# From a planner to an explicit list: the order of the first part of a kernel on one core, with two edits in its start

## The chip, the core and the metric

The kernel runs on one core of one Trainium2 chip: TensorE (PE, with its weight loads as PEld), VectorE (DVE), ScalarE (ACT), GpSimd (POOL), and SyncE (SP), whose queue issues nearly all transfers. The metric is device microseconds of one execution.

## What is computed

Three layers in a row. First a delta rule over 768 positions, for 4 batches and 8 heads of width 48; then a feed-forward layer with a hard-swish gate, then a layer of 8 experts of which each token takes the one with the largest logit.

```python
k_n = k / (np.linalg.norm(k, axis=-1, keepdims=True) + 1e-06)
for t in range(S):
    y[:, :, t] = np.einsum('bhd,bhde->bhe', q[:, :, t], state)
    v_old = np.einsum('bhde,bhd->bhe', state, kt)
    state = state + bt[:, :, :, None] * np.einsum('bhd,bhe->bhde', kt, vt - v_old)
h = x @ w_in;  g = h * np.clip(h + 3.0, 0.0, 6.0) / 6.0;  x2 = g @ w_out
out[mask] = gate_w[mask, None] * (np.maximum(x2[mask] @ w1[e], 0.0) @ w2[e])
```

## The kernel before

The positions are cut into 12 steps `s` of 64; each step has two halves `bp` (two batches each), so 24 items `it = 2 s + bp`. Within a step the rule is a triangular system, solved in groups `g` of four items; across steps a state is carried. The kernel has two parts. The first holds the delta rule, and the feed-forward layer's first 7 of 16 blocks for all tokens. The second (from L1459 on) does the other 9 blocks and the experts. Only the first is touched here.

The first part is written as 31 generators, called streams. Each yields its operations one by one (a block of matmuls is one entry), `"need"` entries that hold it until another stream has reached a point, and `"take"` entries that want one of three PSUM banks (L368). The main ones, in the order of the work:

- `kl_stream` loads the keys, `n_stream` (L546) squares them on ScalarE (tile ksq, one buffer), sums the squares on VectorE (`ss`) and makes the norms; `k_stream` (L571) makes `kn` and the block-diagonal pairs `Kbd`, for the first four items on VectorE, later on GpSimd.
- `kt_stream` and `kg_stream` (L591) transpose `Kbd` by DMA; `g_stream` (L603) multiplies keys by keys (block pG, as 64x64 tiles) and copies the result to `Dt` and `MC`.
- `t_stream` (L634), one pass for a group: VectorE transposes `Dt` to `Bt`, GpSimd multiplies `Bt` by beta, ScalarE clears the PSUM tile `Xp`. `s_stream` (L651) solves the triangular system on VectorE in 31 pairs of `sub` and an update of `Xp`. `z_stream` (L668) transposes the result, splits it (`TT`) and multiplies (pZ).
- `chain(bp)` (L827) carries the state: pR (from the second step on), pW twice, pS, each followed by operations on ScalarE and VectorE. `p_stream` and `o_stream` make pP and the output pO, `x_stream` (L909) transposes it (pX) to `xT`; `xo_stream` stores it on SP.
- `m_stream` (L1029) is the feed-forward part: for each step 7 blocks `ph` of 9 matmuls (three entries), each followed by ScalarE `t`, VectorE `tmin` (it writes the tile t again), ScalarE `gH`, GpSimd `gL`, then `py` of 6 matmuls (two entries).
- `wi_stream`, `wo_stream` narrow the weights on VectorE (tile nws: five operations a block, four of them on VectorE) with the small matmuls pwt and pwc; `ahead_stream` (L1001) does the same for the first three blocks of the second part (tile nw). `scale_stream` sums the squares of the values.

`drive` (L1078) decides the order. Before, it keeps a clock of the engines (class Clock, L39): a cost for each operation, the times at which tiles are written and read, a model of the clock of TensorE. At each step it takes, among the streams that could begin first, the one with the smallest due time; the due times stand in DUE (L1121), one row for a stream, and TOL (L1120) says how near two starts must be to compete. `pin` (L164) fixes the order so chosen on each engine. On the chip nothing of this runs: it only sets the order of instructions on the engines and of transfers on SP.

Of the kernel before, what the change touches and what calls it, by code (L numbers as in the profile page):

```python
# [38 lines left out]
class Clock:  # L39


    def __init__(self, tc):
        self.tc, self.last = tc, {}
        self.free = dict(pe=0.0, act=0.0, dve=600.0, pool=3100.0, dma=0.0)
        self.columns = {}
        self.written, self.read, self.bus, self.issue = {}, {}, 0.0, 0.0
        self.slot, self.count, self.parts = {}, {}, {}
        self.runs, self.phase, self.tick, self.warm = [], 0.0, 0, False
        self.mode = 128, False
        self.place, self.end = {}, dict(act=0.0, dve=0.0)  # L50

    def tile(self, pool, shape, dt, tag, bufs, name):
        t = pool.tile(shape, dt, tag=tag, name=name, bufs=bufs)
        n = self.count[tag] = self.count.get(tag, -1) + 1
        self.slot[t.name] = (tag, n % bufs)
        return t

    def keys(self, ap):

        n = ap.name  # L60
        if n in self.parts:
            return [(n, x) for x in self.parts[n](ap)]
        return [self.slot.get(n, n)]

    def cost(self, op):

        n = 1
        for d in (op.ins[0] if "reduce" in op.fn.__name__ else op.out).shape[1:]:
            n *= d
        if "dma" in op.fn.__name__:  # L70
            return 40
        half = (op.ins[-1] if op.eng == "pe" else op.out).dtype in (FP16, FP32R, BF16)
        if op.eng == "pe":
            if op.ins[-1].dtype == FP32R:
                return n / 2.2
            if op.ins[-1].shape[0] <= 64:
                return max(32 if op.ins[-1].shape[0] == 64 else 25.2, n / 2.4) / op.tiles
            return max(25.5, n / 2.4 + 2.5) if half else 0.85 * max(n, 128)
        fn = op.fn.__name__
        pointers = sum(x.free_size() == 1 for x in op.ins[1:])  # L80
        if op.eng == "act":
            return (52 if op.ins[0].space == PSUM else 109) + 95 * (pointers > 0) + 84 * (len(op.outs) > 1) + 0.836 * n
        if op.eng == "dve":
            if half and fn == "tensor_copy":
                return 64 + 0.26 * n
            if fn == "memset":
                return 60 + (0.38 if half else 0.82) * n
            if fn == "transpose":
                return 70 + 1.06 * n
            if fn == "reciprocal":  # L90
                return 70 + 6 * n
            if fn == "tensor_scalar" and op.ins[0].space != PSUM:
                return 66 + 0.52 * n + 60 * (pointers > 0)
            return 70 + (0.52 if all(x.dtype == FP16 for x in op.ins) else 1.04) * n + 60 * (pointers > 0)
        if op.eng == "pool":
            if fn in ("memset", "tensor_copy"):
                return 80 + 0.81 * n
            wide = op.out.dtype == FP32R or op.out.shape[-1] == 32
            return 60 + (2.5 if wide else 2.15) * n
        raise ValueError(op.eng)  # L100

    def places(self, op):

        r, w = {}, (op.out.space, op.out.start_partition())
        for x in op.ins:
            r.setdefault(x.space, x.start_partition())
        return r, w

    def held(self, op):

        r, w = self.places(op)
        now = self.place.setdefault(op.eng, ({}, {}))
        return any(now[0].get(m, x) != x for m, x in r.items()) or now[1].get(w[0], w[1]) != w[1]

    def shared(self, op):

        if op.eng != "dve" or op.fn.__name__ in ("memset", "transpose", "tensor_reduce", "reciprocal"):
            return False
        wide = [x for x in op.ins if x.free_size() > 1]
        sb = [x for x in wide if x.space != PSUM]  # L120
        if op.fn.__name__ in ("tensor_copy", "tensor_scalar"):
            return bool(sb) and op.out.space != PSUM
        return len(sb) > 1

    def unshared(self, t):

        for a, b in reversed(self.runs):
            if b < t:
                break
            if a <= t:  # L130
                return b
        return t

    def matmul(self, op, t):

        n, tick = op.out.free_size(), int((t + self.phase) * 3 / 10240)
        rows = op.ins[-1].shape[0]
        half = op.ins[-1].dtype in (FP16, FP32R, BF16)
        while self.tick < tick:
            self.warm = self.columns.get(self.tick, 0.0) >= (3060 if self.warm else 3350)  # L140
            self.tick += 1
        self.columns[tick] = self.columns.get(tick, 0.0) + n * (1 if half else 2) * rows / 128
        mode, last = (32 if rows <= 32 else 64 if rows <= 64 else 128, op.ins[-1].dtype == FP32R), self.mode
        self.mode = mode
        turn = 90 * (mode[0] != last[0]) + (0 if mode[1] == last[1] else 85 if mode[1] else 13)
        if self.warm:
            return turn + self.cost(op)
        if rows <= 64:
            return turn + max(53.4 if rows == 64 else 42, n / 1.2) / op.tiles
        return turn + (max(27, n / 1.2) if half else 1.7 * max(n, 128))  # L150

    def ready(self, tiles):
        return max([self.free["pe"]] + [self.written.get(k, 0.0) for x in tiles for k in self.keys(x)])

    def start(self, ops):
        t = 0.0
        for op in ops:
            t = max([t] + [self.read.get(k, 0.0) for x in op.outs for k in self.keys(x)] + [self.written.get(k, 0.0) for x in op.ins for k in self.keys(x)])
        t = max(self.free[ops[0].eng], t + {"pe": 54, "pool": 77}.get(ops[0].eng, 33))
        if ops[0].eng in self.end and "dma" not in ops[0].fn.__name__ and self.held(ops[0]):  # L160
            t = max(t, self.end[ops[0].eng] + 13)
        return self.unshared(t) if self.shared(ops[0]) else t
# [9 lines left out]
    def emit(self, ops):  # L172
        t = t0 = self.start(ops)
        for op in ops:
            t += self.cost(op) if op.eng != "pe" else self.matmul(op, t)
            self.pin(op)
        self.free[ops[0].eng] = t
        if "dma" in ops[0].fn.__name__:
            o = ops[0].out
            n = 2 if o.dtype == FP16 else 4  # L180
            turn = "transpose" in ops[0].fn.__name__
            rate = 200 if turn else 170 if n * o.shape[-1] < 512 else 320
            for d in o.shape:
                n *= d
            self.issue = max(self.issue, t) + 600
            self.bus = max(self.bus, self.issue + 650) + n / rate
            if turn:
                self.free["dma"] = self.bus - 870
            elif ops[0].eng == "dma":
                self.free["dma"] = self.issue  # L190
            t = self.bus + 1900
        else:
            if ops[0].eng == "pool":
                if self.runs and t0 - self.runs[-1][1] < 60:
                    self.runs[-1][1] = t + 55
                else:
                    self.runs.append([t0, t + 55])
            t += {"pe": 165, "dve": 84, "act": 95, "pool": 45}[ops[0].eng]
            if ops[0].eng in self.end:
                r, w = self.places(ops[0])  # L200
                now = self.place.setdefault(ops[0].eng, ({}, {}))
                now[0].update(r)
                now[1][w[0]] = w[1]
                self.end[ops[0].eng] = t
        for op in ops:
            for now, used in ((self.written, op.outs), (self.read, op.ins)):
                for k in [k for x in used for k in self.keys(x)]:
                    now[k] = max(now.get(k, 0.0), t)
# [13 lines left out]
def kernel(ctx: ExitStack, tc: tile.TileContext, q, k, v, beta, w_in, w_out, w_gate, w1, w2, out):  # L222
# [137 lines left out]
    with ExitStack() as ax:  # L360
# [717 lines left out]
        def drive(streams):  # L1078
# [6 lines left out]
            def step(x):  # L1085
                while True:
# [4 lines left out]
                    if x[0] != "next":  # L1091
                        break
# [537 lines left out]
```

## Time and profile before

| | us |
|---|---|
| median of three runs | 999.73 |
| lowest, highest | 997.82, 1004.11 |
| the profiled execution | 1003.64 |
| its span, first to last instruction | 1001.9 |
| from the start to L1459 (end of the first part) | 507.6 |

The profile page gives busy times of the engines over the span, and a table of 40 slices. [...] A releaser called "issue" means that the engine waited for nothing that the profile shows.

### The profile page before, as it was taken

The page shows a single profiled execution, that of the slowest core. Times are in us where ns is not written, and L with a number is a line of the kernel's source. Part 1 is how long each engine was busy: PE and PEld are TensorE (multiplying, and loading weights), DVE is VectorE, ACT ScalarE, POOL GpSimd, SP SyncE. Part 2 cuts the span into 40 slices and gives each one's busy share as a digit, 9 for nine tenths or more (in the row PEclk, how much of TensorE's full clock was granted, in tenths as well). Part 3 has the DMA queues.
Part 4 walks back from the last instruction along what each step waited for, and adds up shares of the span by engine and source line. Part 5 has one row for each costly group of instructions (what it writes and reads, how often), then busy time and mean ns, then how long its engine had stood idle before and what let it go on. Part 6 is the DMA issues. An engine that isn't in the chain of part 4 may idle for free.

```text
span 1001.9 us, 27659 instructions
## 1 busy us (share of the span) xinstructions
PE 885.3 (88%) x11454; PEld 819.2 (82%) x11454; DVE 586.2 (59%) x1611; ACT 569.0 (57%) x1195; POOL 433.2 (43%) x446
## 2 busy tenths in 40 slices
PE   1423898889988899999989999999999999999997
PEld 1412888889888798888878899898899999999996
DVE  7888997888979789653487545554534211222221
ACT  4757889779888876755557333323334542455521
POOL 5255565455546524423343204223104936755761
PEclk9999799999999989999999999999999999999999
DMA  7978797996998956566365432332116734434500
GB/s 127 190 145 158 126 179 135 176 139 124 211 198 110 200 112 123 125 155 208 118 218 172 131 93 97 128 96 97 53 61 240 228 105 153 147 114 141 172 21 20
DMA packets 255080, 138.89 MB, mean 139 GB/s; under 512 B 199587, under 2 KB 239845, under 8 KB 254944
## 3 DMA queue, kind: packets, MB, share of 16 engines
q1 hardware_dynamic: 247120, 118.82, 53.5%
q0 software_dynamic: 7280, 17.41, 5.2%
q8 instruction: 91, 1.49, 0.6%
q10 hardware_dynamic: 544, 0.80, 0.2%
q14 instruction: 45, 0.37, 0.1%
HBM read 71.56 MB, written 35.50 MB: 107 GB/s over the span
## 4 chain that ended last, share of the span: by engine, by line
PE 61%; DVE 14%; ACT 8%; issue 7%; DMA 6%; POOL 4%; SPq 0%; POOLq 0%; ACTq 0%
PE ph L1459 11%; PE ph L1250 9%; PE py L36 5%; PE ph L36 5%; PE py L1475 3%; PE py L1474 3%; PE py L1473 3%; PE pz L1238 3%; PE pz L1240 3%; PE pz L1239 3%; DMA KG<-Kbd 2%; DVE Xp L36 2%; DVE sub L36 2%; PE pO L36 2%; PE pW L36 2%
## 5 line engine op out<-in xcount | busy, mean ns | idle before, releaser
L1254 DVE SCALAR_TENSOR_TENSOR hL<-ph,hH 128x384 fp32r<-128x384 f32 (+6 forms) x64 | 36.1, 564 | 163.6 <-ACT hH L1253 163.6
L36 POOL TENSOR_TENSOR gL<-t,gH 128x256 fp32r<-128x256 f32 x84 | 64.6, 769 | 130.8 <-ACT gH L36 122.6
L1253 ACT ACTIVATE hH<-ph 128x384 fp32r<-128x384 f32 (+6 forms) x64 | 31.6, 494 | 104.8 <-PE ph L1250 104.8
L1462 ACT ACTIVATE t<-ph,half 128x512 f32<-128x512 f32 x54 | 37.1, 687 | 76.4 <-PE ph L1459 75.2
L36 PE MATMUL ph<-xTH,wiH 128*128 128x256 f32 x252 | 76.4, 303 | 4.3 <-DVE t L36 3.4
L1419 POOL DMA_INDIRECT slots<-row,di x24 | 23.9, 997 | 125.1 <-DVE di L1411 119.7
L1463 DVE SCALAR_TENSOR_TENSOR t<-t,ph 128x512 f32<-128x512 f32 x54 | 37.1, 686 | 62.8 <-ACT t L1462 62.5
L1238 PE MATMUL pz<-a2H,hH 128*128 128x384 f32 (+1 forms) x216 | 73.2, 339 | 0.4 <-ACT hH L1253 0.4
L36 PE MATMUL ph<-xTL,wiH 128*128 128x256 f32 x252 | 72.2, 286 | 0.7 <-DVE xTL L36 0.7
L1240 PE MATMUL pz<-a2H,hL 128*128 128x384 f32 (+1 forms) x216 | 72.4, 335 | 0.0
L1239 PE MATMUL pz<-a2L,hH 128*128 128x384 f32 (+1 forms) x216 | 72.4, 335 | 0.0
L36 PE MATMUL ph<-xTH,wiL 128*128 128x256 f32 x252 | 71.6, 284 | 0.0
L1271 POOL DMA_INDIRECT out_dram<-yo,rw x29 | 28.0, 967 | 100.7 <-ACT yo L1270 96.5
L1467 DVE TENSOR_TENSOR gL<-t,gH 128x512 fp32r<-128x512 f32 x54 | 47.5, 882 | 32.6 <-ACT gH L1466 32.5
L36 DVE TENSOR_TENSOR Xp<-Xp,sub 128x31 f32<-128x31 f32 (+15 forms) x186 | 64.0, 344 | 2.8
L36 PE MATMUL py<-woH,gH 128*128 128x392 f32 x168 | 64.9, 386 | 0.7 <-issue 0.7
L36 DVE TENSOR_TENSOR sub<-Bt,Xp 128x31 f32<-128x31 f32 (+15 forms) x186 | 61.6, 331 | 2.2
L298 POOL TENSOR_TENSOR a2L<-r,a2H 128x384 fp32r<-128x384 f32 x64 | 62.5, 1009 | 0.0
L36 ACT ACTIVATE t<-ph,half 128x256 f32<-128x256 f32 x84 | 39.6, 471 | 38.4 <-PE ph L36 31.4
L298 POOL TENSOR_TENSOR a1L<-r,a1H 128x512 fp32r<-128x512 f32 x48 | 60.4, 1305 | 0.1
L36 PE MATMUL py<-woH,gL 128*128 128x392 f32 x168 | 58.7, 350 | 0.7 <-POOL gL L36 0.6
L36 DVE SCALAR_TENSOR_TENSOR t<-t,ph 128x256 f32<-128x256 f32 x84 | 35.0, 417 | 40.3 <-ACT t L36 39.3
(318 smaller groups left out, 3141.9 us busy)
## 6 DMA issues: line engine op xcount, KB each, us to landing
r<-in_moe_w_dram SPq DMA_DIRECT2D x32, 768.0 KB, 4.6
slots<-zrow SPq DMA_DIRECT2D x8, 784.0 KB, 6.2
stage<-in_moe_w_in_dram SPq DMA_DIRECT2D x16, 384.0 KB, 3.9
stage<-in_moe_w_out_dram SPq DMA_DIRECT2D x16, 384.0 KB, 3.2
row<-ypart SPq DMA_DIRECT2D x6, 784.0 KB, 4.5
ysave<-row SPq DMA_DIRECT2D x6, 784.0 KB, 3.9
rw<-slots SPq DMA_DIRECT2D x24, 196.0 KB, 3.1
kr<-in_k_dram SPq DMA_DIRECT2D x24, 192.0 KB, 4.6
```

The source lines that it names most:

```text
L36: return self.fn(*self.a, **self.k)
L298: in_order(pool.tensor_tensor(dst[1], src_ap, dst[0].bitcast(FP32), ALU.subtract))
L1238: pe.matmul(o, hh[:, ts_], a2[0][:, fp], start=fp == 0, stop=False)
L1239: pe.matmul(o, hh[:, ts_], a2[1][:, fp], start=False, stop=False)
L1240: pe.matmul(o, hl[:, ts_], a2[0][:, fp], start=False, stop=fp == KF2 - 1)
L1250: pe.matmul(ph, a1[a][:, c, fs], xt[x][:, c, 0:n], start=k == 0, stop=k == 3 * KD - 1)
L1253: act.activation(hH, ph, ACTF.Relu)
L1254: dve.scalar_tensor_tensor(hL, ph, 0.0, hH.bitcast(FP32), ALU.max, ALU.subtract)
L1459: pe.matmul(ph, wi(a, f)[:, c], xt[x][:, c], start=n == 0, stop=n == 3 * KD - 1)
L1462: act.activation(t_, ph, ACTF.Relu, bias=half, scale=1.0 / 6.0)
L1463: dve.scalar_tensor_tensor(t_, t_, 1.0, ph, ALU.min, ALU.mult)
L1467: dve.tensor_tensor(gL, t_, gH.bitcast(FP32), ALU.subtract)
```

## The change

The class Clock becomes Order, which keeps only `tile`, `pin` and `emit`, and the due times become a list: one character for each entry, 2998 in all, naming the stream whose next entry is issued. `need` entries are stepped over as soon as they hold, a `take` is done when its stream's next character comes. The list was found by a search in which the pieces of TensorE's program count as a resource. Two operations in the start change: the tile that holds the first squares, and the engine of the first multiplication of `Bt`. The products of keys keep their 64x64 tiles.

```diff
-class Clock:
+class Order:
     def __init__(self, tc):
         self.tc, self.last = tc, {}
...
     def emit(self, ops):
-        t = t0 = self.start(ops)
         for op in ops:
-            t += self.cost(op) if op.eng != "pe" else self.matmul(op, t)
             self.pin(op)
...
-            yield "take", lambda: clk.ready(inputs) if freeb else None
+            yield "take", lambda: freeb or None
...
-                    sq_ = tmp([128, H, D], FP32, "ksq", 1)
+                    sq_ = tmp([128, H, D], FP32, "ksq" if g or j % 2 else "vsq")
...
-                yield POOL.tensor_tensor(Bt, Bt, bY[:, g].unsqueeze(1).to_broadcast([128, 32, 32]), ALU.mult)
+                yield (POOL if g else DVE).tensor_tensor(Bt, Bt, bY[:, g].unsqueeze(1).to_broadcast([128, 32, 32]), ALU.mult)
...
+            for n in range(len(streams)):
+                step(n)
+            settle()
+            for n in [ALPHABET.index(c) for c in "".join(ORDER)]:
+                if isinstance(now[n], tuple):
+                    assert now[n][0] == "take" and now[n][1]() is not None, (n, now[n])
+                    step(n)
+                assert isinstance(now[n], list), (n, now[n])
+                clk.emit(now[n])
+                step(n)
+                settle()
+            assert not any(now), now
+
+        ALPHABET = "0123456789abcdefghijklmnopqrstu"
+        ORDER = [
+            "jjaaaajkjkkkpbrbbbbbbkpbbrqqsrpobsrbrbrbqsbsbqsqrjsqbqqqqnsqrqsosposqr1n1n0nr0onsnosrrnnrsnqrsnnqqso",
...
+            "uuttututtttuutututuuuututtttttttuttttttttt8ututtttutut9tutttuttttuttutttutttuttutuuttttuuttttutu988",
+        ]
```

The characters stand for the streams in the order of the call of `drive`: 0 and 1 chain, 2 and 3 wc, 4 and 5 o, 6 ql, 7 qt, 8 xo, 9 yo, a kl, b n, c kg, d kt, e q, f p, g x, h t, i z, j and k zero (GpSimd, VectorE), l s, m g, n k, o beta, p v, q scale, r wi, s wo, t m, u ahead.

## Rows read from the trace of the kernel before

**Rows 1.** The page: busy us by engine; TensorE's program queue (packets, MB, share).
```profile
PE 885.3 (88%) x11454; PEld 819.2 (82%) x11454; DVE 586.2 (59%) x1611; ACT 569.0 (57%) x1195; POOL 433.2 (43%) x446
...
q8 instruction: 91, 1.49, 0.6%
```

**Rows 2.** Busy time by stretch: PE, PEld, DVE, ACT, POOL; clock, DMA share, GB/s.
```profile
88.00:124.00 36.00, 24.82 (x713) 23.35 (x714) 30.52 (x88) 28.61 (x55) 19.85 (x17) 0.83 0.84 143
124.00:482.00 358.00, 330.18 (x7516) 308.83 (x7516) 278.65 (x819) 278.41 (x603) 162.99 (x163) 0.98 0.81 154
482.00:508.00 26.00, 22.52 (x132) 19.03 (x131) 14.75 (x40) 13.24 (x32) 10.17 (x13) 0.93 0.44 140
508.00:1002.00 494.00, 483.96 (x2710) 447.48 (x2708) 189.37 (x440) 196.37 (x389) 198.46 (x206) 0.99 0.39 125
...
197.00:200.50 3.50, 3.50 (x55) 3.24 (x49) 3.27 (x9) 2.64 (x9) 0.00 (x0) 0.51 0.78 247
...
487.00:491.00 4.00, 4.00 (x19) 4.00 (x19) 0.59 (x2) 1.10 (x3) 1.01 (x3) 0.57 0.98 302
```

**Rows 3.** The same view, from the start to two points on VectorE.
```profile
0.00:36.13 36.13, 8.83 (x100) 7.45 (x102) 26.90 (x88) 17.44 (x42) 17.00 (x23) 1.00 0.83 144
...
0.00:87.09 87.09, 23.86 (x389) 20.46 (x389) 72.02 (x226) 51.52 (x119) 41.70 (x48) 1.00 0.83 150
```

**Rows 4.** Groups of VectorE instructions, 0 to 51.2 us: busy us, mean ns, idle before.
```profile
L36 DVE CAST W<-idq 32x256 f16<-32x256 f32 x8 | 3.1, 389 | 0.1
...
L36 DVE SCALAR_TENSOR_TENSOR MC<-pG,MC 128x256 f16<-128x256 f32 x4 | 1.7, 424 | 0.6 <-ACT MC L36 0.5
...
L36 DVE TENSOR_SCALAR eiv<-eiv 128x1 int32<-128x1 int32 x6 | 0.9, 149 | 0.1
```

**Rows 5.** Instructions in order of time: start, us, engine, operation [idle before <-releaser].
```profile
8.88 0.52 ACT L36 ACTIVATE ksq<-kr 128x384 f32<-128x384 f32 x1 [0.62 <-DVE padb L1433]
...
49.70 1.24 DVE L36 STREAM_TRANSPOSE Bt<-Dt 128x1024 f32<-128x1024 f32 x1
...
51.19 2.35 POOL L36 TENSOR_TENSOR Bt<-Bt,bY 128x1024 f32<-128x1024 f32 x1
...
53.57 0.18 DVE L36 TENSOR_TENSOR sub<-Bt,Xp 128x31 f32<-128x31 f32 x1
...
59.95 1.33 DVE L36 TENSOR_SCALAR nws<-nws 128x384 int32<-128x384 int32 x2
```

**Rows 6.** Waits of TensorE, 124 to 482 us: us in total, times, longest.
```profile
PE pW L36 <- issue: 1.8, 1, 1.8
...
PE py L36 <- issue: 0.7, 1, 0.7
```

**Rows 7.** The chain that ended last: start, us, what.
```profile
191.15 1.63 PE pO L36 x96
...
487.30 2.06 PE ph L36 x9
...
491.08 1.02 PE ph L36 x9
```

**Rows 8.** Instructions in order of time, 482 to 508 us: TensorE, then SP, VectorE.
```profile
483.52 0.38 PE L36 MATMUL ph<-xTH,wiH 128*128 128x256 f32 x1 [0.64 <-ACT xTH L36]
...
486.47 0.83 PE L36 MATMUL pwc<-wg,wt 128*128 128x8 f32 x6 [0.69 <-ACT wt L36]
...
504.16 0.52 PE L36 MATMUL pwt<-ident,nw 128*128 128x128 f32 x3 [0.87 <-DVE nw L36]
...
507.59 0.50 PE L1459 MATMUL ph<-xH,wi0H 128*128 128x512 f32 x1 [0.91 <-ACT yp L36]
...
484.50 1.27 SPq L36 DMA_DIRECT2D stage<-in_moe_w_in_dram  x1
...
503.14 0.41 DVE L36 SCALAR_TENSOR_TENSOR t<-t,ph 128x256 f32<-128x256 f32 x1
```

More of the change, by code (lines that the diff above doesn't have):

```diff
@@ L36, in now @@
         return self.fn(*self.a, **self.k)
-class Clock:
+class Order:
     def __init__(self, tc):
         self.tc, self.last = tc, {}
[L44 to L50, printed above, removed]
-    def tile(self, pool, shape, dt, tag, bufs, name):
[L53 to L162, printed above, removed]
@@ L395, in read @@
                 return self.pr
-        clk = Clock(tc)
+        clk = Order(tc)
         def ring(name, n, cols=128):
@@ L1078, in drive, with step @@
         def drive(streams):
-            st = []
-            for n, (gen, due) in enumerate(zip(streams, DUE)):
-                due = [float(x) for x in due.split()]
-                st.append([None, due, n, gen, due.pop(0)])
-            def step(x):
+            now = [None] * len(streams)
+            def step(n):
+                now[n] = "next"
+                while now[n] == "next":
+                    now[n] = next(streams[n], None)
+                if now[n] is not None and not isinstance(now[n], (tuple, list)):
+                    now[n] = [now[n]]
@@ L1086, in step, with settle @@
+            def settle():
                 while True:
-                    x[0] = next(x[3], None)
-                    if x[0] is None:
-                        st.remove(x)
+                    go = [n for n, x in enumerate(now) if isinstance(x, tuple) and x[0] == "need" and x[1]()]
+                    if not go:
                         return
-                    if x[0] != "next":
-                        break
-                    x[4] = x[1].pop(0) if x[1] else x[4]
-                if not isinstance(x[0], (tuple, list)):
-                    x[0] = [x[0]]
@@ L1097, in start @@
-            def start(x):
-                y = x[0]
-                if isinstance(y, tuple):
-                    ok = y[1]()
-                    return ok if y[0] == "take" and ok is not None else -1.0 if ok else None
-                return clk.start(y)
-            for x in list(st):
-                step(x)
-            while st:
-                ready = [(start(x), x[2], x) for x in st]
-                ready = [x for x in ready if x[0] is not None]
-                assert ready, [x[3].__name__ for x in st]
-                t, _, x = min(ready, key=lambda y: y[:2])
-                if isinstance(x[0], list):
-                    eng = x[0][0].eng
-                    end = t + TOL * sum(clk.cost(o) for o in x[0])
-                    same = [y for y in ready if isinstance(y[2][0], list) and y[2][0][0].eng == eng and y[0] <= end]
-                    t, _, x = min(same, key=lambda y: (y[2][4], y[0]))
-                    clk.emit(x[0])
-                step(x)
@@ L1120 @@
-        TOL = 0.041028
-        DUE = [
[31 rows of a table removed]
+                    for n in go:
+                        step(n)
[8 more added lines that the diff above has]
+                clk.emit(now[n])
+                step(n)
+                settle()
```

64 lines of the change are left out of this document (30 added, 34 removed), and 31 rows, old and new, of the table DUE.

## Prediction

> **What bounds the kernel now.** I read the page first. TensorE (PE) is busy 885.3 us of the 1001.9 us span, VectorE (DVE) 586.2, ScalarE (ACT) 569.0 and GpSimd (POOL) 433.2 [rows 1]: over the whole span TensorE is the engine to look at. Then the busy time by stretch [rows 2, 3]. The change only orders the first part, which ends where L1459 begins, at 507.6 us. Behind it TensorE is busy 483.96 of 494 us, and nothing of that is touched. The first part has three stages. Up to 87.09 us, where the first triangular solve ends (32 rows, 31 pairs of operations on VectorE), VectorE is busy 72.02 us and TensorE only 23.86: VectorE and the chain through it set the time. From 124 to 482 us TensorE is busy 330.18 of 358, so it is the limit there, and only 27.8 us are not its own. [...]
>
> The work of TensorE is the same in both lists. I counted the new list entry by entry and set it against the order in which the trace shows the same operations: 666 TensorE entries, 1152 of VectorE (1151 before), 772 of ScalarE, 228 of GpSimd (229 before), 178 transfers on SP. An entry is one operation, or one block of matmuls. So the change can only give back idle time, low-clock time, and the head start of some 90 us; it can't remove work.
>
> **The change, part by part.** *The planner goes* (class Clock's costs, DUE, TOL). It ran while the program was built; on the chip it costs nothing, so 0 us. `take` no longer compares times; the same banks are taken in the order of the list: 0 us, unless a bank comes back later than the list supposes, which then shows as a TensorE wait.
>
> *Two edits in the start.* The first four squares alternate between two tiles, ksq and vsq. Before, the second square waited 0.62 us at the end of a stretch in which the first was reduced, though its data had come [rows 5]; the fourth is like it, so 2 x 0.62 = 1.2 us on the way to the first norm at most. The key loads also move ahead of the first weight load on SP, which only helps. Then the multiplication of the first Bt goes from GpSimd to VectorE. On GpSimd it took 2.35 us (51.19 to 53.54), and the first `sub` started at 53.57, right behind it; VectorE filled the time with norm reductions, so it was not lost. No row shows this multiplication on VectorE. The bounds are the VectorE transposition of the same 128x1024, 1.24 us, and GpSimd's 2.35 us [rows 5]; I take 1.24, the same engine and size. VectorE is the limit of this stage, so this edit by itself is a cost of 1.2 to 2.4 us, paid for by not waiting for GpSimd.
>
> A VectorE operation can be held while GpSimd works: two `nws` operations at 59.95 us took 1.33 us together [rows 5]. [...]
>
> *The order of the start.* In the trace 88 VectorE instructions start before the fourth `kn` (36.14 us), three of them constants outside the list, so 85 entries; the new list has 60 there. Before the transposition that ends the first solve it was 226, or 223 entries, and is now 207 [rows 3]. What leaves are 17 entries: three copies `W<-idq` at 389 ns, one MC at 424 ns, thirteen small ones, at the least 149 ns each [rows 4], together 3 x 0.389 + 0.424 + 13 x 0.149 = 3.5 us; the multiplication comes in. Net 3.5 - 1.24 = 2.3 us less (1.2 with 2.35). But these operations are only later: ahead of the first `tmin` of m_stream, the start of the steady stage, the lists have 315 and 319 VectorE entries, so most of it is paid back where VectorE is busy 30.52 of 36 us [rows 2]. I take 1.5 us of gain. Bounds: 0, if all is paid back; 5 us, if the earlier `kn` (25 entries) also shortens the 15 us in which VectorE idled up to 87 us [rows 3].
>
> *The middle, 124 to 482 us.* For each pair of dependent TensorE blocks I laid the blocks between them end to end, at the durations that the chain gives (such as 96 matmuls of pO in 1.63 us) [rows 7]. From pX to the first `ph` of the same step the list before has three places under 1.2 us, the new one none. From a `ph` block to its `py` thirteen places are under 2.3 us before and six after. The other pairs (pW to pW, pW to pS, pS to pR, pG to the next pG) stay as tight, within 1.5 us in the sum. The shortfalls add up to 1.1 us (pX, without the last step) and 1.2 us (`ph`). I take 1.5 us. Bounds: a gain of 9 us, a third of the 27.8 us; a loss of the same size, since VectorE's order differs much and a late `t` or `uL` shows on TensorE. On SP no transfer moves by more than 11 places; where one that waits for its tile now stands ahead of a transposition of keys, pG waits for it, and the bound holds that too.
>
> *TensorE's program.* The page shows 91 packets of 1.49 MB on the instruction queue, 16 KB each, for 2 x 11454 instructions [rows 1]: about 252 per piece. In the middle TensorE waited for nothing visible ("issue") four times (1.8, 1.3, 0.9 and 0.7 us, 4.7 in all; first and last shown) [rows 6]. I cut both lists every 256 instructions and laid them out at the same durations: of 68 pieces four are shorter than 2.9 us before, seven after (shortest 2.24 and 2.08 us). So the pieces don't become longer; I count 0 for them. The bounds are the 4.7 us gained and a rival below.
>
> *The tail.* Here the lists differ plainly. Before, all `py` of step 10 run ahead of the last pX, and the first `ph` of step 11 finds TensorE idle for 0.64 us; the new list leaves three `py` entries (1.6 us) behind that pX. Then pwc waits 0.69 us for `wt`; the new list has two `ph` entries between pwt and pwc. Behind this idling nine `ph` took 2.06 us from 487.3 us on, against 1.02 at 491 us [rows 7]: the lower clock of that stretch [rows 2], which cost some 1.5 us with the `py` between. At the end pwt waits 0.87 us and L1459 0.91 us [rows 8]. The weight loads for the last block of ahead_stream stand behind the last `xd` stores on SP and were issued at 484.50 us; the narrowing they feed held the last `t` on VectorE until 503.14 us [rows 8]. The new list issues both loads ahead of these stores and narrows before the last two `tmin`; pwt and pwc get `py` entries between them. Sum: 0.64 + 0.69 + 0.87 = 2.2 us idle, half of the 1.5 us of the lower clock, and 0.5 for the late `t` give 3.5 us. Bounds: 1 us (only the plain idle of pX goes), 5 us (all of it and the low clock).
>
> **The sum.** 1.5 + 1.5 + 0 + 3.5 = 6.5 us. The profiled execution took 1003.64 us (span 1001.9 and 1.7 around it), so 997.1 us. The median of the three runs is 999.73, 3.9 lower than the profiled one, so I predict 993.0 us, with 989 to 999 as this case's own range. About 1% (10 us) is what a measurement of this kernel can tell from no change.
>
> **Rivals.** *The middle goes too* (faster). If the list saves a third of the 27.8 us (9 us in place of 1.5) and one stretch of the lower clock with it (1.7), the total is 6.5 + 7.5 + 1.7 = 15.7 us from 1003.64, or 984 on the median's scale. For it: the waits there are many and small, on VectorE's order, and almost half of VectorE's entries changed places. Against it: the TensorE distances hardly grew. *Nothing is carried* (no change): the start is paid back, and only the plain idle of the tail goes, 1 to 2 us: 998 to 1000. For it: equal counts at the first `tmin`. *The pieces stall* (slower). [...] A wait costs up to 1.8 us [rows 6]. Behind the longest one the clock fell, and the 3.5 us from 197 us on ran at 0.51 [rows 2], which costs half of that, 1.7 us; together 3.5 us. With 6.5 us gained elsewhere it ends 10 us slower if five of the seven short pieces stall so, beyond what stalls today: 999.7 + 10 = 1010. For it: seven short pieces instead of four. Against it: of the four short ones today not each stalled by 1.8 us. [...]
>
> **How the numbers follow.** My case 0.45; the middle too 0.34; nothing carried 0.13; pieces 0.08. Faster by over 1% (under 989.7) is the second case and a little of the first: 0.36. Slower is the last: 0.08. The rest, 0.56, is within 1%. The range, 982 to 1004, leaves out most of the slow case and the far end of the fast one.
>
> **What would show it.** Right: the last `XT` transposition of the first solve starts 1 to 5 us before 87.1; L1459 starts at 499 to 503 us instead of 507.6; no 0.69 and 0.87 us waits before pwc and pwt in the tail; TensorE idle between 124 and 482 us still over 20 us; the span behind L1459 as before, 494 us. Wrong: TensorE's idle time in the middle under 18 us (faster), or "issue" waits over 12 us (slower), or new waits for transposed keys (pG, pP) in place of those removed.

## The result, and the profile after

On the chip on which the three times before were taken, the changed kernel took 992.61 us in the median of seven executions and the kernel before 1000.3 in seven; the ratio is 0.9897, with a 95% interval of 0.9875 to 0.9919. On a second chip (below) it was 0.9904, 0.9879 to 0.9929. So the change brings about 10 us by the ratios (7.7 and 11.0 by the medians), where 6.5 had been forecast from 999.73; the 993.0 us came out within half a microsecond of the first median. Where one execution of a kernel below lay far outside the others (1433.39 us, one of twelve of the new start alone; 3140.56 us, one of seven of the spread list), its median and ratio are those of the rest.

The profiled execution took 993.86 us (span 992.1) against 1003.64 (span 1001.9). From the page of after, the engines' busy time and the first of the `ph` groups of the first part (busy us, mean ns of one | idle time ahead and what ended it):

```profile
PE 884.6 (89%) x11454; PEld 817.0 (82%) x11454; DVE 594.8 (60%) x1612; ACT 568.6 (57%) x1195; POOL 430.7 (43%) x445
...
L36 PE MATMUL ph<-xTH,wiH 128*128 128x256 f32 x252 | 76.9, 305 | 14.4 <-DVE t L36 13.7
```

TensorE's work is the one of [rows 1] (885.3 us). The second line was 4.3 us of idle time before, 3.4 of it for `t`: a wait has grown. The view by stretch is cut at the same marks in the kernel after: the last transposition of the first solve, the first `ph`, the last pX, the start of the second part (L1459 before, L1296 in the shorter file after). The mark at the last pX is good to 0.2 us. Columns as in [rows 2]; the clock there is the granted share of TensorE's full clock, and what is called the lower clock is a share of 0.50 in every such stretch of the profile before and the first one after.

```profile
0.00:84.19 84.19, 23.69 (x389) 20.66 (x389) 74.74 (x211) 49.16 (x112) 38.62 (x45) 1.00 0.89 155
84.19:122.31 38.12, 25.59 (x711) 23.67 (x712) 36.98 (x103) 31.25 (x63) 18.21 (x16) 0.82 0.88 152
122.31:471.50 349.19, 326.90 (x7516) 304.67 (x7513) 280.88 (x824) 278.27 (x603) 166.25 (x166) 0.99 0.80 160
471.50:496.25 24.75, 22.14 (x136) 18.42 (x136) 14.68 (x40) 13.47 (x31) 9.54 (x16) 0.96 0.42 128
496.25:992.10 495.85, 486.27 (x2710) 449.55 (x2710) 187.53 (x438) 196.43 (x388) 198.12 (x204) 0.99 0.38 123
```

And the same marks in the kernel before, for the last three stretches (there, too, from the first `ph` on):

```profile
123.57:482.39 358.82, 331.00 (x7522) 309.62 (x7519) 279.28 (x821) 279.12 (x604) 163.38 (x163) 0.98 0.81 154
482.39:507.59 25.20, 21.73 (x128) 18.31 (x126) 14.13 (x39) 12.83 (x30) 9.78 (x13) 0.93 0.44 142
507.59:1001.90 494.31, 484.37 (x2710) 447.84 (x2710) 189.78 (x441) 196.40 (x389) 198.46 (x206) 0.99 0.39 125
```

The first solve ends 2.9 us earlier (87.09 in [rows 3]), but the first `ph` only 1.3. The middle is 9.6 us shorter; 1.6 of these are the three `py` entries that now stand behind the last pX, so 8.0 are won. The tail is 0.45 shorter with these 1.6 us of work more, so 2.0 are won. Together 11.3 us at the start of the second part; the second part is 1.5 longer in this execution, and 9.8 remain.

In the middle TensorE's idle time (length less busy) falls from 27.8 to 22.3 us. What it waits for has changed altogether. First before, then after (columns as in [rows 6]):

```profile
PE ph L36 <- DVE t L36: 3.4, 5, 1.4
PE pP L36 <- DMA QTb<-Qs: 2.6, 3, 1.4
PE pG L36 <- DMA KG<-Kbd: 2.5, 3, 1.6
PE pW L36 <- DVE uL L36: 1.9, 3, 1.1
...
PE pR L36 <- DVE Spr11L L36: 1.4, 2, 0.8
PE pR L36 <- DVE Spr10L L36: 1.4, 2, 0.8
```

```profile
PE ph L36 <- DVE t L36: 12.7, 15, 1.9
PE pZ L36 <- issue: 1.8, 2, 1.6
```

The waits for transposed keys and queries (KG, QTb, KTb) and for the state (Spr) are gone; `ph` now waits for the `tmin` of the `ph` block before it, fifteen times. The kernel has one tile for both halves of `ph`, and a block starts only when the `tmin` of the one before has read the tile: over the 83 pairs of blocks of the first part, the first matmul never starts less than 0.05 us after that `tmin` ends, in either kernel. Where little else stands on TensorE between two blocks, it waits. So the list removed some 16 us of waits for keys, queries, the state and other operands, and brought 9 of `ph` for `t`.

### The profile page after: what moved, and what is told of

It is laid out like the page before. It is cut to its first block, busy times and chain, and to the rows that moved or that the text cites. A ratio compares the mean times of both kernels' runs of the same rounds, so it can differ in the third digit from the quotient of the medians.

```text
span 992.1 us, 27636 instructions
## 1 busy us (share of the span) xinstructions
PE 884.6 (89%) x11454; PEld 817.0 (82%) x11454; DVE 594.8 (60%) x1612; ACT 568.6 (57%) x1195; POOL 430.7 (43%) x445
## 4 chain that ended last, share of the span: by engine, by line
PE 64%; DVE 18%; issue 6%; ACT 6%; POOL 3%; DMA 1%; SPq 1%; POOLq 0%; ACTq 0%; DVEq 0%
PE ph L1296 11%; PE ph L1087 9%; PE ph L36 7%; PE py L36 6%; PE py L1312 4%; PE py L1311 4%; PE py L1310 4%; PE pz L1075 3%; PE pz L1077 3%; PE pz L1076 3%; PE pO L36 3%; DVE Xp L36 2%; DVE sub L36 2%; PE pW L36 2%; DVE nws L36 1%
## 5 line engine op out<-in xcount | busy, mean ns | idle before, releaser
L36 PEld LDWEIGHTS ph<-xTH,wiH 128*128 128x128 f32 x252 | 47.5, 189 | 24.4 <-DVE t L36 24.1
L1087 PE MATMUL ph<-yTL,a1H 128*128 128x384 f32 (+5 forms) x168 | 58.3, 347 | 0.0
```

Source lines behind the costliest of these rows:

```text
L36: return self.fn(*self.a, **self.k)
L1087: pe.matmul(ph, a1[a][:, c, fs], xt[x][:, c, 0:n], start=k == 0, stop=k == 3 * KD - 1)
```

## Experiments

All lists below are orders of the same 2998 entries, written into the changed file, and so have both edits unless it is said otherwise. "Old" is the order that the planner of the kernel before gave. An order is cut at the first `ph` and at the last pX: start, middle, tail. A seam is a place where the old and the new order meet in one list.

**First: does one section carry the gain?** Four kernels on one chip, with 35 executions of the kernel before (median 1001.22 us).

The old order, written out (the first line of 30):

```diff
-            "jjaaaajkjkkkpbrbbbbbbkpbbrqqsrpobsrbrbrbqsbsbqsqrjsqbqqqqnsqrqsosposqr1n1n0nr0onsnosrrnnrsnqrsnnqqso",
+            "rkaakakajkppkrpkjpsojbobbjbbbjbbbqjqqqqqrbqrbrsbqrobsrbqsrrqoooobsbsnsqonqssqs1snr10sqr0sqrsspornpqr",
...
```

> The list of entries is the order that the planner of the kernel before gave, written out; of the change only the two edits (squares in two tiles, first Bt product on VectorE), the loss of the planner and the moved first loads stay. Theory (the gain is in the order, most of it in the middle): within 1.5 us of before, ratio 0.9985 to 1.0015; the last transposition of the first solve within 1.5 us of 87.1. Rival (the edits in the start carry the start's gain): that transposition 2 us or more earlier and 1 to 2 us off the time.

Measured: 1001.46 us, ratio 0.9993 (0.9975 to 1.0011). The last transposition of the first solve started at 88.06 us, 1.0 later than before. (In this profile TensorE was granted 0.50 from 40.7 to 105.5 us; that isn't the cause: two profiles below with the same start and 1.00 there have it at 87.78 and 87.91.) So taking the planner out and making the two edits is worth nothing that can be told from zero, and in the old order the start pays for the edits.

The new start alone (the lists part in the seventh line):

```diff
-            "gs2sc1ls0gnfl1egaa0dl0e1tltnt0s8tnn8lsltl01m0lltetmmpt1lsct0ltntmnmtnmtelpttbttt0sltl1smltl14mfnltlb",
+            "gs2sc1ls0gnfl1egaa0dl0e1nnfllnllmtmlmtdlmsmtlmsbmtltl80b8lts0tttc1tlb0t10et1ln0e4t10l1bsnlp4ltt7nltl",
...
```

> New order for all entries up to the first ph (624 of 2998), the order of before for the rest; with the two edits. Theory: the first ph starts 1.3 us earlier (122.3 against 123.6), the rest as before, in all 1 to 2 us, ratio 0.998 to 0.999; middle from first ph to last pX 358.8 us as before. Rival (the middle's gain is the start's head start, carried on by the other engines): middle 353 us or less, ratio 0.993 or lower.

Measured: 1004.52 us, ratio 1.0039 (1.0018 to 1.0061), slower than before. Neither expectation: the first `ph` came at 121.40 us, 3.3 earlier than in the run before this one, and yet the kernel lost. The instructions around this point, first TensorE, then ScalarE, then VectorE (columns as in [rows 5]):

```profile
121.40 0.39 PE L36 MATMUL ph<-xTH,wiH 128*128 128x256 f32 x1
...
126.30 0.38 PE L36 MATMUL ph<-xTH,wiH 128*128 128x256 f32 x1 [2.95 <-DVE t L36]
...
122.40 1.53 ACT L36 ACTIVATE Dt<-pG 32x256 f32<-32x256 f32 x4
...
124.78 0.46 ACT L36 ACTIVATE t<-ph,half 128x256 f32<-128x256 f32 x1
...
124.08 1.18 DVE L36 SCALAR_TENSOR_TENSOR nws<-stage,nws 128x384 int32<-128x384 int32 x1
125.18 0.41 DVE L36 SCALAR_TENSOR_TENSOR MC<-pG,MC 128x256 f16<-128x256 f32 x1
125.51 0.41 DVE L36 TENSOR_TENSOR sub<-Bt,Xp 128x256 f32<-128x256 f32 x1
125.84 0.41 DVE L36 SCALAR_TENSOR_TENSOR t<-t,ph 128x256 f32<-128x256 f32 x1
```

The head start is lost within one block. The first `ph` ended by 122.8 us, but its `t` stood on ScalarE behind `Dt` and MC, and its `tmin` on VectorE behind weights and the solve, in the order that belonged to the old start; the second `ph` waited 2.95 us. In its second profile (below) it was 3.46. In the changed kernel a block of pW and one of pG stand between the two, and the second `ph` starts at 125.04 us without a wait.

The new middle alone, the old order at both ends (nine lines differ from the new list: the first six are those of the old order above; the seventh, in which the middle begins):

```diff
...
-            "gs2sc1ls0gnfl1egaa0dl0e1tltnt0s8tnn8lsltl01m0lltetmmpt1lsct0ltntmnmtnmtelpttbttt0sltl1smltl14mfnltlb",
+            "fnl0a5lfl2gld301nlgl0mg101s0e00e1ttt0s8t8st010lltetmmpt1lsct0ltntmnmtnmtelpttbttt0sltl1smltl14mnltlb",
...
```

> Order of before up to the first ph and behind the last pX; between them the same entries in the new order; with the two edits. Theory (the middle's order itself carries most of the gain): from first ph to last pX 349 to 352 us instead of 358.8, ratio 0.990 to 0.993; waits of TensorE for transposed keys and state vectors gone, new waits of ph for t some 10 us. Rival of the prediction's sum (1.5 us in the middle): 357 us, ratio 0.998 or higher.

Measured: 999.2 us, ratio 0.9985 (0.9964 to 1.0006). The section itself is 352.15 us long, as the theory said within a little, and its waits are those of the changed kernel, the first line below. The second line, a wait for the state, ended at 122.0 us, ahead of the section:

```profile
PE ph L36 <- DVE t L36: 13.6, 16, 1.9
PE pR L36 <- DVE Spr01L L36: 2.2, 1, 2.2
...
127.14:479.29 352.15, 328.06 (x7480) 305.99 (x7475) 280.22 (x819) 278.78 (x605) 162.97 (x163) 0.99 0.79 156
```

But it begins at 127.14, 2.4 us later than with the old order behind the same start (124.72): the new order puts entries ahead of the first `ph` that the old one has behind it, and the 2.2 us of pR stand there. Of the 6.5 us by which the section is shorter than there (358.64) some 4 are left at the last pX (479.29 against 483.36). The theory fell as to the time: the order of the middle does not bring its gain by itself.

The new tail alone (29 lines differ; the last of them, in which the tail begins):

```diff
...
-            "1tututtt1tttfutttt08t8tut1ttutttttttttuf0uutttttttttu4utttft81tu1t4ttttttttt9tttgu5ggutu5gtttgtguttt",
+            "4t1t1tututututtuttutttttttttuttututttttttttttttttttttttttttttttttttututututg5gt5guuuuuuuugtttgtguttt",
...
```

> Order of before for the entries that stand ahead of the last pX in the new list, the new order behind it (109 entries, three py among them); with the two edits. Theory (what the profiles show: 2.0 us won between the last pX and the second part, 1.5 lost just behind it): start of the second part 1.5 to 2.5 us earlier, the whole 0 to 2 us, ratio 0.998 to 1.000. Rival (the prediction's tail): start of the second part 3.5 us earlier, span behind it 494 us as before, ratio 0.9965.

Measured: 1002.55 us, ratio 1.0023 (1.0002 to 1.0044). No gain, against both expectations; against the old order written out it is 0.003 more with intervals of 0.002 each, which is at the edge of what can be told. In its one profile (998.02 us, the shortest of twelve) the tail took 25.69 us with the three `py`, against 23.76 with the old order written out: no gain either.

**Second: two sections together.** New theory: start and middle belong together, as what one puts off the other must place. Four kernels on another chip; before 1000.44 us there.

> The changed kernel, for comparison on this chip. All theories: ratio 0.988 to 0.992, as measured before.

Measured: 989.46 us, ratio 0.9904 (0.9879 to 0.9929), as expected. Its profiled execution, in three of its stretches:

```profile
121.59:470.19 348.60, 327.21 (x7519) 304.53 (x7515) 281.45 (x825) 277.92 (x603) 165.87 (x166) 0.99 0.79 161
470.19:494.23 24.04, 21.43 (x136) 17.94 (x134) 14.52 (x40) 13.41 (x31) 9.53 (x16) 1.00 0.42 126
494.23:986.80 492.57, 482.54 (x2710) 446.95 (x2710) 187.00 (x438) 196.33 (x388) 198.35 (x204) 1.00 0.39 124
```

The middle is 0.6 us from the first profile's, the second part 3.3 shorter: its 1.5 us of loss in the first profile are not the change's.

Old start, new middle and tail (seven lines differ from the new list, the first again that of the old start; not shown a third time):

> Order of before for the entries up to the first ph, the new order for all the rest; with the two edits. Theory 1 (the middle's gain hangs on the new start, which the middle alone did not have): no better than the middle alone, ratio 0.997 to 0.999. Theory 2 (the gains stand apart, and the seam at the last pX cost the middle alone its gain): ratio 0.991 to 0.994.

Measured: 995.94 us, ratio 0.9962 (0.9944 to 0.9981), between the two expectations, met by neither, nearer theory 1. Putting the old start in costs 5.8 us.

New start and middle, old tail (two lines differ):

```diff
-            "1tututtt1tttfutttt08t8tut1ttutttttttttuf0uutttttttttu4utttft81tu1t4ttttttttt9tttgu5ggutu5gtttgtguttt",
+            "1tututtt1tttfutttt08t8tut1ttutttttttttuf0uutttttttttu4utttft81tu1t4ttttttttt9tttgu5ggutu5ttttgtg9g8t",
...
```

> The new order up to the last pX, the order of before for the 109 entries behind it; with the two edits. Theory 1 (start and middle belong together): nearly the whole gain, ratio 0.990 to 0.993. Theory 2 (the seam at the last pX costs as much as the middle brings): ratio 0.997 or higher, start of the second part no earlier than 501 us.

Measured: 992.46 us, ratio 0.9926 (0.9907 to 0.9944): theory 1. The first `ph` starts at 120.80, the last pX at 471.40, the second part at 494.96 us.

So, all with the old tail and both edits, each against the kernel before on its own chip (the fourth number is from the second chip):

| | old middle | new middle |
|---|---|---|
| old start | 0.9993 | 0.9985 |
| new start | 1.0039 | 0.9926 |

The new start costs 4.6 us ahead of the old middle and gains 5.9 ahead of the new one. If the sections added up, the fourth number would be 1.0031; it is 0.0105 below that, with an interval of some 0.004 (four intervals of 0.002 put together). That is as much as the whole gain.

The tail has some part in it too: with the old start, the new tail cost 3.0 us behind the old middle (0.9993, 1.0023) and gained 2.3 behind the new one (0.9985, 0.9962), each at the edge of its intervals. So a price of the seam at the last pX, theory 2 of the run with the old start, is not excluded, and how much of the interplay is the two half lists' own seams is not shown.

**Third: can the new wait be filled?** 21 moves in the new list put entries of `m_stream` behind the next block of another stream where little stood between two `ph` (15 lines differ):

```diff
-            "gs2sc1ls0gnfl1egaa0dl0e1tltnt0s8tnn8lsltl01m0lltetmmpt1lsct0ltntmnmtnmtelpttbttt0sltl1smltl14mfnltlb",
+            "gs2sc1ls0gnfl1egaa0dl0e1tltnt0s8tnn8lsltl01m0lltetmmpt1lsct0ltntmnmtnmtelptb0sll1tttttsmltl14mfnltlb",
...
```

> The changed kernel with 21 moves: where little stands on TensorE between two ph blocks of m_stream, its entries are put behind the next block of another stream, so that the tmin on VectorE has time. Theory (the 12.7 us of ph waiting for t in the middle are the largest wait that is left, and can be filled): these waits fall under 6 us, last pX 5 to 7 us earlier than in the changed kernel, ratio to before 0.983 to 0.986. Rival (TensorE waits elsewhere instead, as the moved blocks and their chains come due later): waits of ph fall, others rise by as much, ratio 0.989 to 0.993.

Measured: 990.37 us, ratio 0.9896 (0.9878 to 0.9915): the rival by the time. Its only profile is of the execution of 3140.56 us; the kernel after the next shows the waits.

A third chip (before 1001.58 us) had two kernels with two PSUM banks for `ph` in the last steps, the first with the new list:

```diff
+                        if nph[0] == 8 * NF1 + 1:
+                            late_ph.append(clk.tile(psA, [128, 2, 512], FP32, "Xp", 1, "ph2"))
-                        ph = phb[:, nph[0] % 2]
+                        ph = late_ph[0][:, nph[0] % 2, 0:256] if late_ph else phb[:, nph[0] % 2]
```

> The changed kernel; from the second ph block of step 8 on, the two halves of ph lie in two PSUM banks (those of Xp, free after the last solve) instead of one. Theory (ph waits for the tmin of the block before only because both halves share one bank): behind 391 us the five waits of ph for t of 4.0 us in all (1.90 the longest) fall under 1 us, the second part starts 2 to 4 us earlier, ratio to before 0.986 to 0.989. Rival (TensorE would wait for the same t a little later, at py for gH or gL): ph's waits go, those of py rise by as much, ratio as the changed kernel, 0.990 to 0.991.

Measured: 989.28 us, ratio 0.9879 (0.9855 to 0.9902). Behind 391 us only one of the five waits went, that of 1.9 us; the others stayed:

```profile
392.85 0.28 PE L36 MATMUL ph<-xTH,wiH 128*128 128x256 f32 x1
...
394.49 0.41 DVE L36 SCALAR_TENSOR_TENSOR t<-t,ph 128x256 f32<-128x256 f32 x1
...
470.55 0.42 DVE L36 SCALAR_TENSOR_TENSOR t<-t,ph 128x256 f32<-128x256 f32 x1 [1.70 <-ACT t L36]
...
471.03 0.39 PE L36 MATMUL ph<-xTH,wiH 128*128 128x256 f32 x1 [0.75 <-DVE t L36]
```

At 392.85 us a block started 2.05 us before the `tmin` of the block before it ended (at 394.90): there, and only there, the two blocks lie in two different tiles (the old one and `ph2`). At 471.03 us both lie in `ph2`, in two banks, and the block waited as ever; of the 83 pairs this one alone starts before that `tmin` ends. So, as far as one pair can show it, it is not the bank that holds `ph` but the tile: a block waits for the reader of the other half of its own tile, in one bank or in two. My theory named the wrong thing, and its gain of 2 to 4 us is not shown: the last pX came at 466.99 us against 470.19, of which 1.7 are put down to the clock (3.4 us at 0.50 in the middle instead of 6.8; half of the difference, an estimate from [rows 7], where nine `ph` take 2.06 us at 0.50 and 1.02 at 1.00), and the ratio can't be told from the changed kernel's 0.9904. Two tiles for `ph` were not tried.

The same with the spread list:

> The list of the run with spread ph blocks and the two banks of the run before in one kernel. The spread list by itself was worth 0.0 to 0.001, and its only profile shows a disturbed execution; here the stretch from 122 to 391 us shows what it does. Theory A (its moves fill the waits of ph, and the moved chains wait as much): ph for t under 5 us there, other waits of TensorE 4 us or more above the 8 us of the changed kernel; time as the run with two banks alone. Theory B (the waits of ph stay, because t is late for other reasons than short filling): ph for t still 9 us or more there.

Measured: 988.99 us, ratio 0.9877 (0.9855 to 0.9898). Its waits of TensorE from 122 to 484 us:

```profile
PE ph L36 <- DVE t L36: 3.4, 7, 1.2
PE pW L36 <- DVE uL L36: 3.2, 5, 1.6
PE pR L36 <- DVE Spr11L L36: 1.9, 1, 1.9
...
PE ptot L36 <- DVE tot L36: 1.6, 1, 1.6
```

Theory A. Summed by kind over 121 to 485 us of each profile (us):

| | keys by DMA | state | `ph` for `t` | issue | other | sum |
|---|---|---|---|---|---|---|
| before | 6.3 | 2.8 | 3.4 | 4.7 | 10.9 | 28.1 |
| new middle alone (the 2.2 ahead of the first `ph`) | 0 | 2.2 | 13.6 | 5.3 | 6.0 | 27.1 |
| old start, rest new | 0 | 0 | 14.8 | 4.7 | 4.1 | 23.6 |
| changed, first profile | 0 | 0 | 13.4 | 5.4 | 3.9 | 22.7 |
| changed, second profile | 0 | 0 | 14.2 | 3.3 | 4.5 | 22.0 |
| two banks | 0 | 0.2 | 12.6 | 3.1 | 4.9 | 20.8 |
| spread, two banks | 0 | 1.9 | 3.4 | 4.2 | 12.3 | 21.8 |

By the last two rows, spreading took 9 us from `ph` and gave 9 back to the recurrence (pW, pR) and what hangs on VectorE, and 1 to "issue": these 21 moves of entries of `m_stream` only chose who waits. Neither variant is shown to beat the changed kernel.

**The edits, in the new list:**

```diff
-                    sq_ = tmp([128, H, D], FP32, "ksq" if g or j % 2 else "vsq")
+                    sq_ = tmp([128, H, D], FP32, "ksq", 1)
...
-                yield (POOL if g else DVE).tensor_tensor(Bt, Bt, bY[:, g].unsqueeze(1).to_broadcast([128, 32, 32]), ALU.mult)
+                yield POOL.tensor_tensor(Bt, Bt, bY[:, g].unsqueeze(1).to_broadcast([128, 32, 32]), ALU.mult)
```

> The new list with both edits undone: all squares in one tile, the first Bt product on GpSimd. Theory (the list of the new start is made for the edits: with the old list they cost 1.0 us at the last transposition of the first solve and gave nothing): first kn 0.5 to 1.2 us later than 18.0, the first sub 1 us or more later than in the changed kernel as nothing else is left for VectorE to do there, ratio to before 0.991 to 0.994. Rival (the edits are worth nothing in either list): first solve ends within 0.5 us of 84.3, ratio 0.989 to 0.991.

Measured: 991.43 us, ratio 0.9913 (0.9891 to 0.9935): by the time not to be told from the changed kernel, so neither side is decided by it. The profile goes with the theory: in it the first `kn` is 0.5 us and the end of the first solve 1.5 us later than in the second profile of the changed kernel (85.96 against 84.51), the last pX 1.6 us (471.83 against 470.19). GpSimd, then VectorE without the edits, then VectorE with them:

```profile
47.09 2.34 POOL L36 TENSOR_TENSOR Bt<-Bt,bY 128x1024 f32<-128x1024 f32 x1 [0.35 <-DVE Bt L36]
...
47.36 2.68 DVE L36 TENSOR_SCALAR nws<-nws 128x384 f32<-128x384 f32 x2
...
51.94 0.17 DVE L36 TENSOR_TENSOR sub<-Bt,Xp 128x31 f32<-128x31 f32 x1
```

```profile
46.82 0.35 DVE L36 TENSOR_SCALAR nws<-nws 128x384 f32<-128x384 f32 x1
47.08 1.22 DVE L36 TENSOR_TENSOR Bt<-Bt,bY 128x1024 f32<-128x1024 f32 x1
48.21 0.35 DVE L36 TENSOR_SCALAR nws<-nws 128x384 int32<-128x384 int32 x1
...
50.47 0.18 DVE L36 TENSOR_TENSOR sub<-Bt,Xp 128x31 f32<-128x31 f32 x1
```

While GpSimd multiplies, two `nws` operations take VectorE 2.68 us instead of 2 x 0.35: it is held for 2.0 us, and doing the product itself costs it 1.22. By these numbers the moved product is a gain of 0.8 us; what holds VectorE is not shown.

**Why is the new start alone so slow?** The same kernel once more for its profile:

> The new start with the rest of the list before, once more for its profile: most of its executions took 1002 to 1008 us, the profiled one 999.5. If one takes 1004 or more: theory A, more waits of TensorE between the first ph and the last pX (34 us or more idle instead of 28.8); theory B, more stretches at the lower clock (each 3.4 us long and worth 1.7) in the same waits; theory C, the difference lies behind the start of the second part.

Measured: 1004.96 us, span 1003.2 against 997.8 in its first profile. Theory A by most of it, just short of its 34 us: idle time of TensorE from the first `ph` to the last pX is 33.4 us against 28.8, of the 5.4 us of difference in the span 4.6. The waits that grew are "issue" (4.2 to 7.2 us) and `ph` for `t` (6.0 to 7.2). Theory B is out: the middle has three stretches of 3.4 us at the lower clock, against four in the first profile. The second part is 1.0 longer. This is one execution.

## Why the prediction was right, and where not

**TensorE's work is the same; only idle time can go.** Right: 885.3 and 884.6 us busy.

**The planner costs nothing.** Right: 0.9993 with the old order written out.

**The two edits.** The product on VectorE was taken at 1.24 us by the transposition of the same size [rows 5] and took 1.22. The first `kn` gained 0.5 to 1.1 us in the new order (18.77 us without the edits, 17.66 to 18.25 in seven profiles with them), where at most 1.2 was forecast, and nothing in the old (19.92 us against 19.80). But the account was on the wrong side: the two `nws` at 59.95 us in [rows 5], 1.33 us together while GpSimd made `Kbd` (58.95 to 61.06 us), were not set against the product on GpSimd, when such a hold is what it costs VectorE where weights are narrowed beside it (the 2.68 us above). In the old order, where norm reductions stood there, the edits cost 0.6 to 1.0 us at the end of the solve (four profiles), a little less than the 1.2 forecast for the product by itself; in the new order they gain 1.5.

**The start.** The last transposition of the first solve was to come 1 to 5 us earlier and came 2.9 earlier; most of it was to be paid back by the first `ph`, which came 1.3 us earlier, 1.5 forecast. Over all profiles the first `ph` stands at 124.1 us with the old start (123.57, 124.72, 124.09) and at 121.6 with the new (seven profiles, 120.80 to 122.31): 2.5 us. What the step didn't have is that this head start is worth something only if the middle goes on from it: with the old middle it is lost in one wait of 2.95 us.

**The middle.** This is the step that went wrong, by its mechanism and not only by its size: 1.5 us forecast, 8.0 measured in the first profile, 8.6 in the second (358.82 against 348.60 and 1.6). The step laid TensorE's blocks end to end and priced the distances of dependent blocks. That sees neither what was removed nor what was added. Removed were waits for transposed keys and queries (6.3 us), for the state (2.8) and 7 us of others: the distances between TensorE's blocks don't give these; that the operands came late by their places on SP and VectorE fits, but no run takes it apart. Added was `ph` waiting for the `tmin` of the block before (3.4 to 13.4 us), a pair of blocks that was not in the list of pairs, since code and planner treat the halves of the tile as two. TensorE's idle time stayed over 20 us, as said; it fell to 22.3, which is 5.5 of the 8; of the rest 1.7 are put down to the clock (10.2 us at 0.50 before, 6.8 after, half of the difference by the same estimate), and 0.8 are not accounted for.

**TensorE's program.** Zero forecast; "issue" came to 5.4 and 3.3 us in two profiles against 4.7. The rival of the stalling pieces is out: in the changed kernel these waits didn't grow beyond their scatter. No run shows that a piece of 256 instructions or one shorter than 2.9 us is what makes TensorE wait: the short ones went from four to seven, and "issue" from 4.7 us to 5.4 and 3.3. What the runs show is this. The 91 packets on the instruction queue have 16384 bytes each, before and after. In the thirteen profiles, each of the 74 "issue" waits of TensorE from 121 to 485 us ended 2.2 to 3.3 us after a fetch (a packet on that queue) had begun, while fetches lie 5.4 to 5.9 us apart (medians). That "issue" is here TensorE waiting for its own program is the author's reading of these times; no run changed the fetches. For the longest wait before, the queue from 192.9 to 196 us (packets, MB, share), with its one fetch from 192.99 us on, then TensorE:

```profile
q8 instruction: 1, 0.02, 2.7%
...
195.82 0.18 PE L36 MATMUL pW<-uL,W 128*128 128x48 f16 x1 [1.85 <-issue]
```

**The tail.** 3.5 forecast, too much. By the profile of the old tail behind the new middle (494.96 - 471.40 = 23.56 us, without the three `py`) against the new one (24.04 with these 1.6 us) it is 1.1 us; the ratios 0.9926 and 0.9904 make it 2.2, within their intervals. Other profiles agree with 1.2 us: the old tail took 23.56 to 23.76 us in five without the lower clock in it, the new one behind the new middle 23.99 to 24.04 in five; behind the old middle it gained nothing (above). The plain idle of 0.69 and 0.87 us ahead of pwc and pwt did go, as said, but new waits came:

```profile
PE ph L36 <- DVE t L36: 1.1, 2, 0.8
PE ph L1296 <- ACT yp L36: 0.6, 1, 0.6
PE py L36 <- ACT gH L36: 0.4, 1, 0.4
PE py L36 <- POOL gL L36: 0.3, 1, 0.3
```

Together with 0.2 us for pwc these are 2.6 us, where 3.5 were idle before. And the lower clock at 487 us [rows 2], half of which was counted as a gain, isn't the tail's: the five other profiles of kernels with the old tail don't have it there. In the first profile after, one stands at the end of the new tail and behind it:

```profile
494.30:501.10 6.80, 6.21 (x15) 4.63 (x15) 1.90 (x17) 2.22 (x6) 4.27 (x17) 0.50 0.78 247
```

By the same estimate (half of the time at 0.50) the 6.21 us of busy time in it cost some 3 us; ahead of it stand the small waits above, and whether they brought it is not shown.

**Behind L1459.** Unchanged, as said: 494.31 before, 495.85 and 492.57 after; the other profiles lie between 492.6 and 495.6 whatever the order. The mean clock was 0.99, 0.99 and 1.00: 3.4 us at 0.50 from 528.2 us on before, 4.85 and 3.4 us (from 496.25 and 518.2 us on) in the first profile after, beside the last 4 us of each, in which TensorE has no work. Elsewhere the two agree: the 466 us from 532 us before and from 522 us after on have 462.25 and 462.36 us of TensorE. That the clock makes the differences is an estimate from these three.

**The signs.** L1459 was to start at 499 to 503 us; in the two profiles of the changed kernel the second part started at 496.25 and 494.23, earlier than that sign allowed. The others came as said: the end of the solve, no waits of 0.69 and 0.87 us, over 20 us idle in the middle, no new waits for keys.

**The total.** That 993.0 (the sum as it stands gives 993.2) lies so near the first median is luck. Two errors met: the middle was 6.5 too small, the tail some 2 too large, and the sections don't add up by themselves; and the forecast stands on a median of three that was below those of all later series (1000.3 to 1001.58). The gain of 10 lies between the forecast case and the rival "the middle goes too", whose reason (many small waits, on VectorE's order) was the right one; its 9 us were near the 8 measured. Carrying nothing is refuted by the whole list, but no single section brought a gain that can be told from none. That the scatter of single profiles (986.8 and 992.1 for one kernel, 997.8 and 1003.2 for another) is half of the gain speaks for the width of the range.

What stays open: why the new start with the old middle is 4 us slower than before by the ratio, when its seam costs 3 us, the head start brings as much, and its two profiles differ by 5.4 (3 of them "issue"); and whether the interplay has causes besides the seam that the two half lists make.

## What to carry to other kernels

An order of entries that is good as a whole could not be priced section by section here: the new start cost 5 us with the old middle and brought 6 with the new, as each section places what the one before put off. Count the waits by what releases them before counting distances on the busiest engine; a list that removes one kind of wait can bring another (here on a tile in two halves, where in all 83 pairs the next block started behind the `tmin` of the one before), and if that is filled by hand, the wait can go to a third place with the sum unchanged.

## What the runs showed of the hardware

- A tiny VectorE operation can wait out a GpSimd one, and hold what is queued behind it. In the first profile after, VectorE, then GpSimd, then TensorE:

```profile
395.44 1.54 DVE L36 SCALAR_TENSOR_TENSOR tot<-sums,tot 128x1 f32<-128x1 f32 x1
396.91 0.41 DVE L36 SCALAR_TENSOR_TENSOR t<-t,ph 128x256 f32<-128x256 f32 x1
...
394.22 2.75 POOL L36 TENSOR_TENSOR TT<-Bt,TT 128x1024 f16<-128x1024 f32 x1 [4.37 <-ACT TT L36]
...
397.37 0.39 PE L36 MATMUL ph<-xTH,wiH 128*128 128x256 f32 x1 [1.92 <-DVE t L36]
```

  `tot` on 128x1 took 1.54 us, where the shortest of its kind in the middle took 0.22; it ended with the GpSimd product, `t` came late, and TensorE waited 1.92 us, the longest wait for `t` in that profile.
- Two executions of one program run at the lower clock in different places of the middle: the changed kernel at 159.8 and 398.7 us (3.4 us each) in one profile, at 283.2 us (6.8 us) in the other.
- The "issue" waits of one program came to 4.2 us in one execution and 7.2 in another, in the same stretch of the same list; over all profiles such waits end 2.2 to 3.3 us after a fetch began (above).
- A granted clock of 0.50 over 65 us cost nothing that shows. From 40.7 to 105.5 us TensorE was busy 23.05 us at 0.50 (old order written out) and 23.30 at 1.00 (new middle alone, the same entries there); its matmuls pG<-KG took 239 and 238 ns, pwt 438 and 436. Why these are no slower is open.
